# Making the first feed-forward layer's seven weight operands during attention, on ScalarE and GpSimd, instead of at the start of the feed-forward layer

## The chip, the cores and the metric

The kernel runs on one core of a Trainium2 chip. The metric is the device time of one execution in microseconds (us), lower is better. The core's engines work from queues of their own, each strictly in order: TensorE (PE, with its weight loads PEld), VectorE (DVE), ScalarE (ACT), GpSimd (POOL), and SyncE (SP), which here issues nearly all DMA transfers.

## The reference, cut to what matters

One transformer block on 2048 rows of width 512 in fp32: a modulated layer norm, an attention with 32 heads of 16 in four segments of 512 rows (softmax inside the segment plus a linear memory read from the earlier segments), and a feed-forward layer of width 1792.

```python
h = _layernorm(x, axis=-1) * (1 + ca) + sa
x = x + ga * _A_ref(h, A_wq, A_wk, A_wv, A_wo, A_beta)
h = _layernorm(x, axis=-1) * (1 + cb) + sb
x = x + gb * _B_ref(h, B_w1, B_b1, B_w2, B_b2)     # (relu(h @ w1 + b1) ** 2) @ w2 + b2
```

## The kernel before, in words

Precision: each fp32 operand of the large products is split into a rounded part "hi" (type fp32r) and the rest "lo" = value - hi, and a product is three matmuls: hi*hi, hi*lo, lo*hi. A split costs one copy (hi, on ACT) and one subtraction (lo, on DVE or POOL).

Stages. First W_q, W_k and W_v are loaded and split. Then 16 attention units u (four segments s times four groups of eight heads) are worked on: projections (`qk`, `vproj`), a first pass over the scores that finds row maxima (`a_quad`, whose maxima are read by the DVE line 854), a second pass with the exponentials (`b_quad`: ACT line 1035, causal zeroing on POOL line 1022, the product with V on PE line 1077), the linear memory (`mem`), and at the end of each unit a normalization (`norm`, DVE lines 1126 to 1129). The finished output of segments 0 to 2 goes to DRAM; that of segment 3 stays in the SBUF tile `X1L` (four blocks of 512 columns per partition). `X1L` is also where the raw W_q is loaded at the very start; between the two uses it holds nothing. Projecting the attention output (`wo_tile`, lines 1173 to 1208) and the second layer norm (`ln2`) follow, for segments 0 to 2 in between the units of the last segment.

The feed-forward layer runs over the four segments, and in each over seven pairs p of 128-wide blocks of the 1792 hidden columns. Its first product is done with Winograd's form of Strassen's scheme: seven block products instead of eight (`ffn1`, PE line 1470, twelve matmuls of 128x256 for each pair of block products), for which the 2x2 blocks A11, A12, A21, A22 of W1's pair are made into seven operands: A11, A12, A22 and the sums S1 = A21+A22, S2 = S1-A11, S3 = A11-A21, S4 = A12-S2. Each of the seven is split into hi and lo. The seven operands of a pair fill one slot of 1792 KB of the pool "w1", which has two slots. In segment 0 `load_w1` makes them: two loads of 256 KB (SP line 1382), four sums on POOL (line 1398), four copies on ACT (line 1405), four subtractions on DVE (line 1407), and a store of the finished slot to DRAM (`w1_dram`, SP line 1416). In segments 1 to 3 `fetch_w1` (line 1420) reads a finished slot back. W2's blocks are loaded, multiplied by the output gate on POOL (line 1429) and split (ACT line 1430, DVE line 1432) by `load_w2`, also in segment 0 only. The second product is `ffn2` (PE lines 1534 to 1536), whose input is squared and split on ACT and DVE (lines 1506 to 1518).

Order. The Python code makes a list of nodes (`op`, `act`, `dve`, `pe`, `sp`), each with an engine, the nodes that it follows and the buffers that it takes (`get`) and gives back (`put`). The table `ORDER` gives for each engine the sequence in which its nodes are issued, by node number. `Plan.run` only turns this into one emission order; semaphores between engines come from the tiles that the instructions share. `N_FFN` stands for the point where attention's tiles are freed and those of the feed-forward layer are laid over them.

Of the kernel before, what the change touches and what calls it, by code (L numbers as in the profile page):

```python
# [17 lines left out]
P = 128  # L18
# [39 lines left out]
8-16 3 17-33 86 94 34-35 88 36-39 96 111 40-43 105 123 44 117 45-76 171 77 161 172 162-163 173-174 164 175 165-167 176  # L58
168 177-178 328-329 214 330-331 215 333 216 749 217 334 231 335 754 336 239 219-220 252 221-222 487 266 488-489 273
260 490 197 492 198 236 245 493-494 199 242 200 495 202-203 257 248 204-205 357 263 613-615 278 285 276 616 281 371  # L60
288 618 293 619 269 620 378 365 432 621 386 297 383 301 298 764 435 299 304 362 308 368 311 320 316 374 392 516 759
521 558 321 389 437 444 322 561 403 440 768 324 769 447 770 395 771 524 530 452 773-774 537 775 527 776 684 411
456-458 533 545 413 405 460 551 642 687 419 467 463 877 937-938 475 647 939 470 940 656 650 421 427 479-481 429 563
942 542 943 570 944 573 945 578 801 548 802-804 566 653 806 554 807 663 671 808-809 659 582-584 586 483 818 593 819
589 820 677 601 821 1012 835 823 849 824 596 825-826 843 1072 668 1073-1074 880 846 1075 674 1362 605 883 689 1077 692
1078 680 1079 856 870 1080 606 867 696 607 699 840 708 704 1147 712 709-710 852 715 1207 970 1208 719 1209-1210 727
722 1212-1213 864 1214 1015 1215 861 978 873 991 609 731 1005 886 732-733 984 893 1018 896 889 999 735 901 1357 1352
981 1002 905-906 975 909 912 907 996 916 1367 987 919 1105 1113 928 924 1116 929 1008 1119 1150 1021 930 1153 1024
1028 932 1371-1372 1110 1031 1373 1036 1374 1126 1285 1040 1134 1044 1041-1042 1051 1059 1376 1122 1377 1047 1140 1378
1054 1379 1282 1240 1063 1288 1064-1065 1137 1421 1067 1156 1422 1159 1423-1424 1245 1131 1163 1426-1427 1171 1254  # L70
1428 1143 1429 1166 1404-1405 1248 1261 1406 1269 1407 1251 1175-1177 1179 1409 1272 1186 1410 1182 1411 1275 1257
1412 1438 1540-1541 1446 1189 1542-1543 1266 1480 1194 1545-1546 1452 1483 1547-1548 1278 1449 1198-1200 1291 1443
1675-1676 1202 1459 1677 1298 1678 1473 1301 1960 1955 1467 1680-1681 1464 1294 1682 1306 1455 1683 1470 1615 1573
1310-1311 1314 1810 1317 1811 1587 1812 1321 1813 1324 1312 1333 1476 1329 1815 1489 1816 1492 1817-1818 1581 1594
1334 1584 1970 1335 1578 1496 1486 1602 1499 1337 1504 1965 1508 1512 1618 1509 1750 1515 1510 1599 1519 1522 1621
1590 1605 1527 1608 1531 1708 1722 1753 1532 1624 1716 1631 1533 1756 1634 1974 1713 1627 1975 1611 1976 1729 1719
1977 1535 1639 1643-1644 1725 1647 1645 1743 1650 1979 1654 1980 1737 1981 1657 1885 1982 1740 1662 1666-1668 1759
1734 2003 1843 2004 1888 1766 2005 1746 2006 1851 1670 1769 2008-2009 1774 2010 1864 2011 1854 2132 1878 2133 1762
1857 2134-2135 1869 2079 2137 1778-1780 1848 1782 2138 1789 2139 1872 1860 2140 2037 2020-2023 1797 2051 1785
2025-2026 1875 1792 2027-2028 2045 1881 1801 2058 2072 1802-1803 2063 1894 2256 2048 1897 2257 1901 2258 2042 1904  # L80
2259 1805 1909 2261 2069 2262 2054 2263 2066 2182 2264 2203 1913-1915 1917 2187 2380 1924 2381 2193 1932 2382 1920
2383 1927 2190 2385 2075 2386 2161 2196 1936 2166 2082 2387-2388 2175 2085 1937-1938 2169 2089 2092 1891 2101 2097
1940 2105 2102-2103 2108 2112 2115 2172 2327 2120 2522 2124-2126 2178 2285 2299 2296 2128 2525 2532 2526-2528 2206
2209 2535 2213 2199 2536 2542 2537 2306 2293 2216 2538 2545 2290 2221 2311 2546 2552 2547-2548 2225-2227 2229 2320
2236 2555 2562 2556-2557 2232 2244 2239 2558 2565 2317 2302 2566 2602 2567-2568 2409 2417 2414 2248-2250 2330 2423
2337 2605-2606 2572 2333 2345 2314 2607-2608 2575 2340 2252 2323 2576 2612 2577-2578 2430 2420 2438 2349-2351 2444
2353 2356 2615 2582 2616-2618 2585 2360 2441 2363 2586 2368 2435 2426 2587 2643 2588 2622 2647 2372-2374 2454 2457
2461 2625-2627 2447 2464 2376 2469 2655 2592 2628 2473-2475 2477 2484 2480 2595-2596 2451 2487 2492 2597 2632 2598
2496-2498 2635 2651 2500 2636-2638 2662 2672 2692 2682 2665-2666 2685 2667 2686 2695-2697 2687 2668 2885 2688 2698
2882 2886 2883-2884 2675-2676 2888 2887 2905 2677-2678 2911 2906-2908 3046 2910 2909 3044-3045 3048 3050 3043 2928  # L90
# [3 lines left out]
3086 3022 3024 3087 3025 3153 3091-3092 3154 3090 3378 3155 3157 3089 3093 3156 3159 3094 3097-3098 3096 3370 3158  # L94
3095 3102 3177 3174 3176 3175 3105 3108 3179 3374 3099 3178 3180 3201 3196 3302 3301 3197 3195 3300 3305 3198-3199
3306 3200 3218 3217 3216 3304 3303 3312 3220 3318 3307 3310 3219 3314 3221-3222 3317 3238 3237 3239-3240 3308 3321
3241 3316 3319 3323 3320 3322 3327 3324 3243 3242 3259 3326 3260 3258 3330 3325 3261 3329 3263 3328 3331 3334 3262
3382 3338 3280 3282 3264 3335 3279 3281 3333 3332 3283 3336 3284 3339 3337 3342 3340 3344 3413 3410 3285 3346 3639
3341 3411-3412 3348 3343 3414-3415 3350 3345 3635 3354 3347 3416 3362 3432 3436 3433 3349 3431 3351 3434 3631 3355
3353 3435 3437 3352 3453 3452 3454 3457 3365 3627 3455 3359 3356 3560 3456 3458 3474 3558 3475 3473 3559 3562 3479  # L100
3476 3567 3563 3557 3569 3564 3497 3571 3477-3478 3561 3565 3494 3574 3496 3573 3576 3575 3495 3500 3577 3499 3580
3515 3520 3498 3578-3579 3582 3584 3581 3517 3516 3588 3585 3518 3583 3519 3587 3521 3536 3586 3590 3537 3591 3538
# [287 lines left out]
def block_kernel(ctx, tc, x, wq, wk, wv, wo, beta, w1, b1, w2, b2, c, wmod, out):  # L390
# [868 lines left out]
    def h2_ops(s, at):  # L1259
# [20 lines left out]
        for j, name in enumerate(BO):  # L1280
# [311 lines left out]
```

## Time and profile before

| | us |
|---|---|
| median of 3 runs | 802.03 (799.05, 802.03, 803.28) |
| the profiled execution's own time | 803.49 |
| its span, first to last instruction | 801.8 |
| PE busy in the span | 764.7 (95%) |
| DVE, ACT, POOL busy | 624.3 (78%), 445.9 (56%), 302.1 (38%) |
| mean granted TensorE clock | 0.989 |

The shares are means over the whole span. The parts of it that the following speaks of are, in us from the start of the span: the last of the projections' weights, then attention until about 450, segment 0 of the feed-forward layer from 450 to 550, segments 1 to 3 from 550 to 790, and the last output transfer until 802. A row of a table of stretches gives, for each engine, its busy time in that stretch and in brackets its instructions, then the granted clock, the mean busy share of the DMA engines and what they moved. A row of the waits reads "engine tile line <- what ended the wait: us in total, times, longest". A row of groups reads "line engine operation out<-in shape xcount | busy us, mean ns of one | idle time before". A row of one line gives minimum, median and maximum of the duration in ns and the first and last start.

### The profile page before, as it was taken

To read this page: it belongs to the slowest core of one execution; us is meant where nothing else is said; L and a number is where in the kernel's file an instruction comes from. 1 tells how busy PE (TensorE), PEld (TensorE's weight loads), DVE (VectorE), ACT (ScalarE), POOL (GpSimd) and SP (SyncE) were. 2 spreads that over 40 slices of the span, in tenths; PEclk is the share of its full clock that TensorE was granted. 3 is DMA by queue.
4 is the path that set the end of the run, shared out by engine and by line. 5 is a ranking of instruction groups with operands and counts; after the bars stand their busy time and mean duration, and the time that the engine had idled before them with its cause. 6 is when DMAs were issued, how large, how long until landed. Compare 5 with 4: busy or idle time off the path is not lost. (4 is left out here: it accounts for less than half of the span.)

```text
span 801.8 us, 18015 instructions
## 1 busy us (share of the span) xinstructions
PE 764.7 (95%) x6649; PEld 599.8 (75%) x6649; DVE 624.3 (78%) x1619; ACT 445.9 (56%) x1001; POOL 302.1 (38%) x372
## 2 busy tenths in 40 slices
PE   8999999999999999999999898899999999999993
PEld 8886667655877677775666576778998889889882
DVE  5488768788988787999898899999865875657351
ACT  2659767789869986868657545556212321221110
POOL 4735524657636774355132564564002020000000
PEclk9999999999999999999999999999999999999997
DMA  9563661323504333335531455677554463455504
GB/s 297 174 162 97 191 183 56 95 61 85 157 15 116 85 80 84 83 97 153 142 105 51 132 169 216 217 261 301 189 184 160 139 227 120 184 197 184 191 7 183
DMA packets 55345, 116.81 MB, mean 146 GB/s; under 512 B 8277, under 2 KB 25433, under 8 KB 51674
## 3 DMA queue, kind: packets, MB, share of 16 engines
q1 hardware_dynamic: 55106, 115.53, 45.4%
q8 instruction: 53, 0.87, 0.5%
q14 instruction: 34, 0.28, 0.1%
q10 hardware_dynamic: 152, 0.13, 0.1%
HBM read 68.45 MB, written 20.19 MB: 111 GB/s over the span
## 5 line engine op out<-in xcount | busy, mean ns | idle before, releaser
L854 DVE CUSTOM_DVE_ANT_0 ba<-ba,msk 128x384 f32<-128x384 f32 (+2 forms) x384 | 192.1, 532 | 26.5 <-PE ba L849 17.4
L1035 ACT ACTIVATE pt<-bpb 128x512 f32<-128x512 f32 x320 | 172.8, 610 | 27.6 <-PE bpb L1018 23.9
L1470 PEld LDWEIGHTS bh<-H2o,w 128*128 128x128 f32 x1176 | 155.9, 189 | 22.7 <-DVE w L1407 5.0
L1470 PE MATMUL bh<-H2o,w 128*128 128x256 f32 x1176 | 163.6, 283 | 7.6 <-DVE w L1407 3.2
L1022 POOL TENSOR_SCALAR_AFFINE_SELECT pt<-pt 128x512 f32<-128x512 f32 x128 | 81.4, 655 | 120.5 <-ACT pt L1035 78.3
L742 PE MATMUL bqk<-HT,WQK 64*128 64x512 f32 x720 | 103.3, 396 | 0.2
L1516 ACT CAST rr<-xx 128x512 fp32r<-128x512 f32 x56 | 34.5, 620 | 100.8 <-DVE xx L1506 65.3
L1077 PE MATMUL bpv<-pt,VT 128*32 128x512 f32 (+3 forms) x1024 | 82.1, 441 | 3.4 <-POOL pt L1022 3.0
L1018 PE MATMUL bpb<-ST 64*128 64x256 f32 (+2 forms) x512 | 80.3, 353 | 1.4 <-ACT phi L785 0.4
L849 PE MATMUL ba<-ST 63*128 63x256 f32 (+2 forms) x512 | 75.6, 346 | 1.4 <-ACT oraw L1101 0.7
L742 PEld LDWEIGHTS bqk<-HT,WQK 64*128 64x128 f32 x720 | 68.9, 185 | 9.2 <-DVE sg L778 0.6
L1018 PEld LDWEIGHTS bpb<-ST 64*128 64x128 f32 x512 | 51.2, 187 | 26.5 <-issue 5.9
L849 PEld LDWEIGHTS ba<-ST 63*128 63x128 f32 x512 | 49.6, 186 | 22.3 <-DVE mx L854 4.5
L1535 PE MATMUL bpf<-w,rr 128*128 128x512 f32 x160 | 63.0, 394 | 1.6 <-DVE w L1432 1.6
L1534 PE MATMUL bpf<-w,rr 128*128 128x512 f32 x160 | 63.5, 397 | 0.0
L1536 PE MATMUL bpf<-w,rr 128*128 128x512 f32 x160 | 62.8, 392 | 0.7 <-DVE rr L1518 0.7
L1077 PEld LDWEIGHTS bpv<-pt,VT 128*32 128x32 f32 x1024 | 27.3, 109 | 40.3 <-issue 28.9
L815 PE MATMUL bv<-WVO,HT 64*128 64x512 f32 x384 | 54.5, 397 | 0.4 <-ACT WVO L716 0.2
L854 DVE DVE_READ_ACCUMULATOR2_ANT mx<- 128x1 f32 x384 | 54.3, 141 | 0.0
L1518 DVE TENSOR_TENSOR rr<-xx,rr 128x512 fp32r<-128x512 f32 x56 | 42.8, 769 | 12.9 <-ACT rr L1516 12.7
L893 DVE TENSOR_REDUCE mx<-ac 128x4 f32<-128x1024 f32 x32 | 38.9, 1216 | 11.4 <-POOL ac L890 11.3
L1270 POOL TENSOR_TENSOR tt<-h2raw 128x512 f32<-128x512 f32 x8 | 11.9, 1492 | 93.9 <-ACT h2raw L1236 93.9
(175 smaller groups left out, 1439.7 us busy)
## 6 DMA issues: line engine op xcount, KB each, us to landing
w<-w1d SPq DMA_DIRECT2D x21, 1792.0 KB
ST<-sg SPq DMA_DIRECT2D x192, 128.0 KB
w1d<-w SPq DMA_DIRECT2D x7, 1792.0 KB
wr<-in_B_w SPq DMA_DIRECT2D x28, 256.0 KB
xt<-in_A_x SPq DMA_DIRECT2D x16, 256.0 KB
wm<-in_w_mod SPq DMA_DIRECT2D x16, 256.0 KB
xw<-in_A_x SPq DMA_DIRECT2D x16, 256.0 KB
o_dram<-on SPq DMA_DIRECT2D x12, 256.0 KB
```

The costliest lines, as they stand in the source:

```text
L742: nc.tensor.matmul(bank(banks[w]), W3(w, k, x, cols.start, cols.stop)[r], HT[r, y, k], start=turn == k == i == 0, stop=turn == 1 and k == ...
L815: nc.tensor.matmul(bank(banks[t]), HT[r, x, k, (t2 + t) * P:(t2 + t + 1) * P], WVO[r, k, y], start=turn == k == i == 0, stop=turn == 1 and ...
L849: nc.tensor.matmul(dst[:, c0:c0 + n], ST[b:b + 63, 0, sl, qt * P:(qt + 1) * P], ST[b:b + 63, 1, sl, :n], start=True, stop=True)
L854: nc.vector.tensor_tensor_reduce(i, i, msk[:, 512 - n:], scale=1.0, scalar=-3e38, op0=ALU.add, op1=ALU.max, accum_out=o)
L1018: nc.tensor.matmul(dst, ST[b:b + 64, 1, sl, kb * P:(kb + 1) * P], ST[b:b + 64, 0, sl, q0:512], start=True, stop=True)
L1022: nc.gpsimd.affine_select(out=ap, in_=ap, pattern=[[0, ap.shape[1]], [1, P]], compare_op=ALU.is_ge, fill=0.0, base=0, channel_multiplier=-1)
L1035: ns = [act(512, lambda j=j: nc.scalar.activation(buf("PPP"[n], pt)[:, i + j], bank(keys[j]), AF.Exp, scale=0.25), pr[slot] + 0.01 + 0.001 ...
L1077: nc.tensor.matmul(bank(o)[32 * hq:32 * hq + 32, q0:q0 + src.shape[1]], v[:, a:a + 32], src, start=start, stop=stop, tile_position=(0, 32 ...
L1470: nc.tensor.matmul(pb(i), A[:, x, kk], B[:, y, kk], start=kk == j == 0, stop=kk == 1 and j == 2)
L1534: nc.tensor.matmul(q, rh, wh, start=(i == 0), stop=False)
L1535: nc.tensor.matmul(q, rh, wl, start=False, stop=False)
L1536: nc.tensor.matmul(q, rl, wh, start=False, stop=(i == NF - 1))
```

## The change

`load_w1` is gone. `make_w1(p, ...)` is called for all seven pairs ahead of the attention's nodes, and its nodes are placed among those of attention by the new `ORDER`. It works in `X1L`: blocks 0 and 1 hold the pair's two raw loads, blocks 2 and 3 hold hi and lo of the operands being split. For each pair: two loads of 256 KB, four copies on ACT (three of 512 columns, one of 256), four subtractions on POOL (formerly DVE), four sums on POOL (of 256 columns, in place), and four stores to `w1_dram`, of two, one, two and two operands (512, 256, 512 and 512 KB). One raw buffer ("wx") and one output buffer ("wy") exist, so each split waits for the store of the one before, and each pair for the last split of the pair before. In segment 0, `fetch_w1(p, 0, ...)` now reads each slot back, as in the other segments. The normalization of the last segment, which writes `X1L`, waits for all stores. The order of the operands within a slot is changed (S3 ahead of S1). All five sequences in `ORDER` are new; only the node numbers at W1's place and the sequence differ, and no other work is added or taken out.

```diff
 ORDER = {
     "PE": """
...
-             "w1": 2, "w2": 5, "p1": 1, "u2": 2, "u3": 1, "tt": 3, "S": 1}
+             "w1": 2, "w2": 5, "p1": 1, "u2": 2, "u3": 1, "tt": 3, "wx": 1, "wy": 1}
...
+    AO = ("A11", "A12", "A22", "S3", "S1", "S2", "S4")
+    def make_w1(p, pr):
+        raw = [X1L[:, i].rearrange("p (k n) -> p k n", k=KD) for i in (0, 1)]
+        out_ = X1L[:, 2:4].rearrange("p a n -> p (a n)").bitcast(F32R)
+        wx = ("wx", p)
+        ld = [sp(lambda i=i: nc.sync.dma_start(raw[i], w1[:, (2 * p + i) * P:(2 * p + i + 1) * P].rearrange("(k p) n -> p k n", p=P)),
+                 pr, 1 << 18, after=[q for c in range(4) for q in WN[0, c]], get=[("wx", wx)]) for i in (0,)]
...
+        def split(i, a, b, src, deps, put):
...
+            h = act(n, lambda: nc.scalar.copy(flat(0), src), t, sbuf=True, after=deps, get=[("wy", wy)], put=put)
+            l = op("POOL", 1.24 if n == 512 else 0.72, lambda: nc.gpsimd.tensor_tensor(flat(1), src, flat(0).bitcast(F32), op=ALU.subtract), t + 0.07,
+                   after=[h], put=put)
+            W1D[p].append(sp(lambda: nc.sync.dma_start(w1_dram[p][:, :, a:b], view().bitcast(F32)), t + 0.18, n << 10, after=[h, l], put=[wy]))
...
+        def sum_(t, dst, x, y, f, deps):
+            return op("POOL", 0.72, lambda: nc.gpsimd.tensor_tensor(dst, x, y, op=f), pr + 0.07 * t, after=deps)
+        g1 = split(0, 0, 2, whole(0), [ld[0]], [wx])
+        g2 = split(1, 2, 3, blk(1, 1), [ld[1]], [wx])
+        n1 = sum_(12, blk(1, 1), blk(1, 0), blk(1, 1), ALU.add, g2)
+        n2 = sum_(13, blk(1, 0), blk(0, 0), blk(1, 0), ALU.subtract, [n1])
+        n3 = sum_(14, blk(0, 0), blk(1, 1), blk(0, 0), ALU.subtract, [n2, *g1])
+        n4 = sum_(15, blk(0, 1), blk(0, 1), blk(0, 0), ALU.subtract, [n3])
+        split(2, 3, 5, whole(1), [n2, n3], [wx])
+        split(3, 5, 7, whole(0), [n4], [wx])
...
-        ks = [op("DVE", 0.84, lambda j=j: norm(j), p_fin + 0.02 + 0.001 * j, after=[n, n_gate], put=[b[j]]) for j in (0, 1)]
+        ks = [op("DVE", 0.84, lambda j=j: norm(j), p_fin + 0.02 + 0.001 * j, after=[n, n_gate, *(W1L if last else [])], put=[b[j]]) for j in (0, 1)]
...
+    for p in range(NF // 2):
+        make_w1(p, 7.05 + 2.57 * p)
+    W1L = [n for p in W1D for n in W1D[p]]
...
-    def load_w1(p, t0):
...
-            sn[o] = op("POOL", 0.92, lambda o=o, x=x, y=y, f=f: nc.gpsimd.tensor_tensor(blk[o](), blk[x](), blk[y](), op=f), us(t0 - 6 + 0.7 * i),
...
-            l = op("DVE", n / 960 + 0.07, lambda a=a, b=b, src=src: nc.vector.tensor_tensor(
-                w1slot(p, 0)[:, 1, a:b], src(), w1slot(p, 0)[:, 0, a:b].bitcast(F32), op=ALU.subtract), us(t0 - 4.5 + i), after=[h], put=put)
...
-        n = sp(lambda: nc.sync.dma_start(w1slot(p, s).bitcast(F32), w1_dram[p]), us(t0 - 12), 7 << 18, after=[W1D[p]], get=[("w1", key)])
+        n = sp(lambda: nc.sync.dma_start(w1slot(p, s).bitcast(F32), w1_dram[p]), us(t0 - 12), 7 << 18, after=[N_FFN, *W1D[p]], get=[("w1", key)])
...
     for p in range(NP):
-        load_w1(p, STEP * p)
+        fetch_w1(p, 0, STEP * p)
         load_w2(p, STEP * p)
```

More of the change, by code (lines that the diff above doesn't have):

```diff
@@ L222 @@
+2307 2667 2533 2532 2527 2531 2530 2070 2525 2677 2328 2526 2524 2687 2528-2529 2534 2523 2727 2431 2697 2737 2452
+2707 2747 2555 2717 2576 2757 2827 2785 2832 2787 2846 2786 2797 2828 2836 2817 2807 2837 2845 2859 2841 2854 2850
+2855 2863 2908 2864 2868 2886 2872 2882 2873 2881 2877 3174-3180 3431-3437 3688-3689 3392 3690-3691 3138 3386 3692
+3389 3649 3693-3694 3132 3652 3903 3906 3135 3900 3643 3909 3646 3395 3129
 """,
@@ L710, in block_kernel, with whole, blk @@
     clear(2, PR0 + 1.3, [n_w])
+    AO = ("A11", "A12", "A22", "S3", "S1", "S2", "S4")
+    w1_dram = [dram.tile([P, 2, 7, 2, P], F32, name=f"w1d{p}") for p in range(NF // 2)]
+    W1D = {}
+    def make_w1(p, pr):
[4 more added lines that the diff above has]
+                 pr, 1 << 18, after=[q for c in range(4) for q in WN[0, c]], get=[("wx", wx)]) for i in (0,)]
+        ld.append(sp(lambda: nc.sync.dma_start(raw[1], w1[:, (2 * p + 1) * P:(2 * p + 2) * P].rearrange("(k p) n -> p k n", p=P)),
+                     pr + 0.01, 1 << 18, after=[q for c in range(4) for q in WN[0, c]], soft=ld))
+        W1D[p] = []
+        def split(i, a, b, src, deps, put):
+            n, wy, t = (b - a) * 256, ("wy", p, a), pr + 0.14 + 0.5 * i
+            view = lambda: out_[:, :2 * n].rearrange("p (h j k n) -> p h j k n", h=2, j=b - a, k=2)
+            flat = lambda q: out_[:, q * n:(q + 1) * n]
+            h = act(n, lambda: nc.scalar.copy(flat(0), src), t, sbuf=True, after=deps, get=[("wy", wy)], put=put)
+            l = op("POOL", 1.24 if n == 512 else 0.72, lambda: nc.gpsimd.tensor_tensor(flat(1), src, flat(0).bitcast(F32), op=ALU.subtract), t + 0.07,
+                   after=[h], put=put)
+            W1D[p].append(sp(lambda: nc.sync.dma_start(w1_dram[p][:, :, a:b], view().bitcast(F32)), t + 0.18, n << 10, after=[h, l], put=[wy]))
+            return [h, l]
+        def whole(i):
+            return X1L[:, i]
+        def blk(i, j):
+            return X1L[:, i, 256 * j:256 * j + 256]
+        def sum_(t, dst, x, y, f, deps):
[8 more added lines that the diff above has]
+        split(3, 5, 7, whole(0), [n4], [wx])
@@ L1354, in block_kernel @@
     STEP = 10.44
-    W1N, W2N, W1D = {}, {}, {}
+    W1N, W2N = {}, {}
     W2LATE = {3: 0, 5: 1}
-    w1_dram = [dram.tile([P, 2, 7, 2, P], F32, name=f"w1d{p}") for p in range(NP)]
     def wraw(k):
@@ L1376, in w2slot @@
         return TL[k]
-    def load_w1(p, t0):
-        key, ks, sk = ("w1", p, 0), [("wr1", p, i) for i in (0, 1)], ("S", p)
-        raw = [lambda i=i: wraw(ks[i]).rearrange("p (k n) -> p k n", k=KD) for i in (0, 1)]
-        ld = [sp(lambda i=i: nc.sync.dma_start(raw[i](), w1[:, (2 * p + i) * P:(2 * p + i + 1) * P].rearrange("(k p) n -> p k n", p=P)),
-                 us(t0 - 9 + i), 1 << 18, after=[N_FFN], get=[("wr", ks[i])]) for i in (0, 1)]
-        def S():
-            if sk not in TL:
-                TL[sk] = FF["sb"].tile([P, 4, 2, P], F32, name="S", tag="S0")
-            return TL[sk]
-        blk = {"A11": lambda: raw[0]()[:, 0:2], "A12": lambda: raw[0]()[:, 2:4], "A21": lambda: raw[1]()[:, 0:2], "A22": lambda: raw[1]()[:, 2:4],
-               "S1": lambda: S()[:, 0], "S2": lambda: S()[:, 1], "S3": lambda: S()[:, 2], "S4": lambda: S()[:, 3]}
-        f1, f2 = ks
-        prev = None
-        sn = {}
-        for i, (o, x, y, f, put) in enumerate((("S1", "A21", "A22", ALU.add, []), ("S2", "S1", "A11", ALU.subtract, []),
-                                               ("S3", "A11", "A21", ALU.subtract, []), ("S4", "A12", "S2", ALU.subtract, []))):
-            deps = [sn[q] for q in (x, y) if q in sn] + [ld[int(q[1]) - 1] for q in (x, y) if q[0] == "A"]
-            uses = sorted({ks[int(q[1]) - 1] for q in (x, y) if q[0] == "A"})
-            sn[o] = op("POOL", 0.92, lambda o=o, x=x, y=y, f=f: nc.gpsimd.tensor_tensor(blk[o](), blk[x](), blk[y](), op=f), us(t0 - 6 + 0.7 * i),
-                       after=deps, get=[("S", sk)] if i == 0 else (), put=uses)
-        ends = []
-        for i, (a, b, src, n, deps, put) in enumerate(((0, 2, lambda: raw[0]().rearrange("p (j k) n -> p j k n", j=2), 512, [ld[0]], [f1]),
-                                                 (2, 3, lambda: raw[1]()[:, None, 2:4], 256, [ld[1]], [f2]),
-                                                 (3, 5, lambda: S()[:, 0:2], 512, [sn["S1"], sn["S2"]], [sk]),
-                                                 (5, 7, lambda: S()[:, 2:4], 512, [sn["S3"], sn["S4"]], [sk]))):
-            h = act(n, lambda a=a, b=b, src=src: nc.scalar.copy(w1slot(p, 0)[:, 0, a:b], src()), us(t0 - 5 + i), sbuf=True, after=deps,
-                    get=() if i else [("w1", key)], put=put)
-            l = op("DVE", n / 960 + 0.07, lambda a=a, b=b, src=src: nc.vector.tensor_tensor(
-                w1slot(p, 0)[:, 1, a:b], src(), w1slot(p, 0)[:, 0, a:b].bitcast(F32), op=ALU.subtract), us(t0 - 4.5 + i), after=[h], put=put)
-            if i == 0:
-                first = h
-            else:
-                first.outs.append(h)
-                h.left += 1
-            ends.append([h, l])
-        W1N[p, 0] = {"A11": ends[0], "A12": ends[0], "A22": ends[1], "S1": ends[2], "S2": ends[2], "S3": ends[3], "S4": ends[3]}
-        W1D[p] = sp(lambda: nc.sync.dma_start(w1_dram[p], w1slot(p, 0).bitcast(F32)), us(t0 + 1), 7 << 18, after=[q for e_ in ends for q in e_], put=[key])
```

293 lines of the change are left out of this document (146 added, 147 removed), and 17 rows, old and new, of the table ORDER.

## The prediction

> **What bounds the kernel now.** I first cut the span into stages, since the shares of the page mix them. One row is one stretch: its length, then busy time of PE, PEld, DVE, ACT and POOL, granted clock, DMA share, GB/s.
>
> ```profile
> 46.00:375.00 329.00, 321.36 (x3668) 227.33 (x3668) 279.67 (x919) 265.23 (x635) 180.36 (x229) 0.99 0.38 102
> 375.00:450.00 75.00, 74.54 (x618) 49.56 (x614) 65.85 (x184) 49.11 (x106) 22.30 (x37) 1.00 0.38 107
> 450.00:470.00 20.00, 16.31 (x116) 12.54 (x109) 17.58 (x33) 9.55 (x19) 11.53 (x11) 1.00 0.48 130
> 470.00:550.00 80.00, 71.28 (x426) 59.39 (x425) 78.13 (x128) 45.91 (x89) 45.19 (x42) 1.00 0.66 239
> 550.00:790.00 240.00, 237.52 (x1482) 212.64 (x1480) 157.42 (x308) 53.37 (x105) 17.09 (x13) 1.00 0.45 163
> ```
>
> PE is the bound everywhere but in one place. In attention (46 to 450) it idles 7.64 + 0.46 us of 404; in segments 1 to 3 of the feed-forward layer 2.48 us of 240. In segment 0 (450 to 550) it idles 3.69 + 8.72 = 12.4 us of 100, and from 470 on DVE is busy 78.13 of 80 us: that stage is VectorE's. The waits of PE between 450 and 560 say on what:
>
> ```profile
> PE bh L1470 <- DVE w L1407: 3.2, 4, 1.8
> PE bwot L1200 <- DVE X1L L1135: 2.1, 1, 2.1
> PE bwop L1175 <- DVE oT L1208: 1.6, 1, 1.6
> PE bpf L1535 <- DVE w L1432: 1.6, 1, 1.6
> PE bpf L1536 <- DVE rr L1518: 1.2, 3, 0.5
> PE bh L1470 <- DVE xx L1489: 1.1, 2, 0.9
> PE bh L1470 <- DVE H2o L1286: 0.8, 2, 0.5
> PE bh L1470 <- DVE u L1493: 0.6, 1, 0.6
> ```
>
> All eight end on DVE. 3.2 us are W1's subtractions (L1407) themselves, 3.7 us (L1135, L1208) the hand-over from the last attention unit, and 5.3 us other results queued on the full DVE. The groups of 450 to 550 that the change takes out of this stage (L1407, L1405, L1398), and one that stays:
>
> ```profile
> L1407 DVE TENSOR_TENSOR w<-wr,w 128x256 fp32r<-128x256 f32 (+1 forms) x14 | 11.2, 806 | 0.5 <-ACT w L1405 0.5
> L1407 DVE TENSOR_TENSOR w<-S,w 128x512 fp32r<-128x512 f32 x14 | 10.1, 729 | 0.0
> L1405 ACT CAST w<-S 128x512 fp32r<-128x512 f32 x14 | 8.6, 620 | 5.7 <-POOL S L1398 5.7
> L1405 ACT CAST w<-wr 128x512 fp32r<-128x512 f32 (+1 forms) x14 | 7.0, 515 | 4.9 <-DMA wr<-in_B_w 4.8
> L1398 POOL TENSOR_TENSOR S<-wr 128x256 f32<-128x256 f32 x14 | 12.1, 869 | 11.4 <-DMA wr<-in_B_w 7.5 <-DVE h2raw L1238 2.2 <-DVE w L1407 1.6
> L1398 POOL TENSOR_TENSOR S<-wr,S 128x256 f32<-128x256 f32 x7 | 7.0, 1006 | 0.3
> L1398 POOL TENSOR_TENSOR S<-S,wr 128x256 f32<-128x256 f32 x7 | 7.0, 1005 | 2.8 <-DMA wr<-in_B_w 2.5
> L1518 DVE TENSOR_TENSOR rr<-xx,rr 128x512 fp32r<-128x512 f32 x12 | 12.2, 1013 | 0.6 <-ACT rr L1516 0.6
> ```
>
> **The gain in segment 0.** DVE loses 11.2 + 10.1 = 21.3 us, ACT 15.6, POOL 26.1. Of DVE's 95.7 us some 74 are left for 100, less still if the POOL sums slow the rest (L1518's mean is 1013 ns here; over the whole run its median is 685):
>
> ```profile
> L1518 DVE TENSOR_TENSOR rr<-xx,rr x56: 676/685/1787, 481.3 to 782.0; 128x512 fp32r<-128x512 f32 x56
> L778 DVE TENSOR_TENSOR sg<-bqk,sg x32: 679/691/693, 31.6 to 372.7; 128x512 fp32r<-128x512 f32 x32
> ```
>
> At 74%, DVE is about as loaded as in segments 1 to 3 (157.42 of 240, 66%), where PE idles 1%. So I take: the 3.2 us vanish; the 5.3 us shrink to 1.0 (1% of 80 us, rounded up for the W2 blocks still made here), gain 4.3; the 3.7 us of hand-over keep 3.0, since their chain (normalization, transposition, copy, subtraction) stays, and only lines waiting behind L1407 or slowed by L1398 get quicker, gain 0.7. Sum 8.2 us. Bounds: 3.2 if only the direct waits go, 12.4 if all idle time goes. What is late next there is PE itself.
>
> **W1 fetched in segment 0.** Seven stores of 1792 KB and fourteen loads leave the stage, seven fetches of 1792 KB come; less DMA than before in it.
>
> ```profile
> L1382 SPq DMA_DIRECT2D wr<-in_B_w x14: 368/379/459, 447.2 to 539.2; - x14
> L1470 PEld LDWEIGHTS bh<-H2o,w x1176: 186/188/193, 468.3 to 779.0; 128*128 128x128 f32 x196
> 756.00:762.00 6.00, 6.00 (x38) 5.29 (x37) 1.43 (x3) 1.62 (x3) 0.00 (x0) 1.00 0.87 323
> ```
>
> Around the last fetch 323 GB/s were moved, so 1.835 MB take 5.7 us. The first raw load could be issued at 447.2, as attention's tiles came free; a fetch from there lands by about 455, and the first weight load of L1470 is at 468.3. I cost the first fetch at nothing; if its slot lay over tiles freed 10 us later, it would cost about 2 us. The later five wait for a slot, as in segments 1 to 3, where PE's list names no DMA. Zero taken; ends zero and the second rival.
>
> **The price in attention.** The sequences show where the new nodes stand: counted against what ran beside them before, all 28 copies fall between 46 and 340 us, and the last POOL subtraction stands just ahead of the causal zeroing of 366.14. The rows for prices and cover (the two L1077 rows are PE's and PEld's waits of 46 to 375, L1022 the POOL group of that stretch):
>
> ```profile
> L611 POOL TENSOR_TENSOR HT<-lnf,HT x12: 1264/1279/1287, 70.8 to 285.6; 128x512 fp32r<-128x512 f32 x12
> L1398 POOL TENSOR_TENSOR S<-wr x14: 728/784/1181, 457.6 to 544.1; 128x256 f32<-128x256 f32 x14
> L1022 POOL TENSOR_SCALAR_AFFINE_SELECT pt<-pt 128x512 f32<-128x512 f32 x103 | 64.9, 649 | 74.6 <-ACT pt L1035 52.6 <-PE bqk L742 9.0 <-issue 5.9
> PE bpv L1077 <- POOL pt L1022: 2.7, 4, 1.2
> PEld bpv L1077 <- POOL pt L1022: 7.7, 16, 1.4
> 170.00:210.00 40.00, 38.92 (x504) 24.01 (x497) 35.91 (x119) 38.26 (x89) 25.02 (x36) 0.96 0.31 88
> 250.00:290.00 40.00, 39.35 (x490) 25.74 (x489) 32.48 (x106) 38.66 (x90) 29.22 (x39) 1.00 0.29 74
> ```
>
> - POOL: 21 subtractions of 512 columns at 1.279 us (L611, same shape), 7 of 256 and 28 sums at 0.784 (L1398's median): 26.9 + 5.5 + 22.0 = 54.3 us. POOL goes from 180.36 to 235 us of 329, 55% to 71%. Its queue is in order, and behind each new instruction stand zeroings of exponentials (L1022) that L1077 reads. The new work fills 54.3/329 = 16.5% of the time, so 103 zeroings lose on average half of 1.28 us in 16.5% of cases, 10.9 us in all; 20 of the 103 were waited for by PE or its weight loads before, so a fifth reaches PE: 2.1 us. Ends: zero (the sequence may put the new work into the 74.6 us in which POOL sat idle ahead of L1022) and all 10.9.
> - ACT: 21 copies at 0.62 us and 7 at about 0.4 (L1405: 515 mean over both sizes): 15.8 us, 265.23 to 281 of 329. Two stretches have no room: 3 copies (1.6 us) fall into 170 to 210, where ACT has 1.7 us left, and 4 (2.3 us) into 250 to 290, where it has 1.3. The overflow there is 1.0 us; I take 0.9, ends zero and the 3.9 us of all seven.
> - SP and DMA: 42 issues of 0.379 us are 16 us of a queue that carries the operand copies for the score products; each store waits for its subtraction, and all issues behind it wait too. The new traffic, 3.7 + 12.8 MB at 323 GB/s, is 51 us of wire in 329. PE's list of 46 to 375 names no DMA, so slack is there; I take 0.3, ends zero and 3.
> - The last segment's normalization waits for the last store. Its first start was 380.6; the last store follows 366.14 by 1.28 + 0.38 us of work and issue and 1.6 us of wire (512 KB at 323 GB/s), near 370. Ten us of cover: zero. Were that gone, DVE would stand with the maxima (L854) behind it, and PE after them.
>
> ```profile
> 366.14 2.94 POOL L1022 TENSOR_SCALAR_AFFINE_SELECT pt<-pt 128x512 f32<-128x512 f32 x3 [0.87 <-ACT pt L1035]
> L1129 DVE TENSOR_TENSOR X1L<-bfin,dn x8: 423/424/425, 380.6 to 456.4; 128x256 f32<-128x256 f32 x8
> L1128 DVE TENSOR_TENSOR dn<-dn,omg x32: 174/176/1269, 88.1 to 455.7; 128x16 f32<-128x16 f32 x32
> ```
>
> - POOL against DVE: L1518 (both inputs in SBUF, one shape) spreads from 676 to 1787 ns, L778 (one input in PSUM) stays within 679 to 693. In attention nearly all of DVE's time is on PSUM inputs; the exposed line is L1128, 176 ns at the median and 1269 at most. PE's list has no wait on its chain there, so: zero. The Trainium skill's page "SBUF — State Buffer", section "Who interferes with whom", speaks against the change here: a VectorE instruction with two SBUF inputs and a GpSimd instruction that reads SBUF exclude each other for a whole instruction. The two ranges above agree with it. By it some 24 of the L1128 would each meet a subtraction in 16.5% of cases and lose 0.64 us, an estimate of 2.5 us on DVE; if PE took all of that, the sum would come out at 799.6 and not 797.1.
> - The new sequences themselves: no row prices them. PE's switches between operand shapes are as many as before (174 against 175 by the two tables). Zero, and part of the range.
>
> Sum: -8.2 + 2.1 + 0.9 + 0.3 = -4.9 us. The profiled execution took 803.49, 1.5 above the median; against it the change gives 798.6, against the median of 802.03 it gives **797.1**. Half a per cent, about what a measurement here can tell from no change, is 4.0 us: faster means below 798.0, slower above 806.0.
>
> **The rivals.**
> - *All of the idle time goes and attention hides everything* (near 791): 12.4 less 1 to 2. For it: POOL's 74.6 idle us ahead of the zeroings, and DVE's relief. Against it: the hand-over chain and the full ACT stretches.
> - *The gain turns into a wait for fetched slots* (802 to 803). A slot is free only after its pair's seven products, and then takes 5.7 us, with 512 KB of W2 loads (1.6 us) sharing the wire. If each of the five later fetches comes 1.0 us late, 5 us are lost and nothing is left of the 4.9; at 1.2 us it is 803. Against it: in segments 1 to 3 the same slots do, though without W2's loads.
> - *POOL sets attention's pace* (slower, near 807). The queue is in order and VectorE, ACT and PE are all over 80% busy beside it. If every one of the 56 new instructions held PE up by 0.22 us, 12.3 us would be lost in place of 3.3, less 8.2: 806. It decides above that; at 0.15 us each there is no change. For it: from 170 to 210 and from 250 to 290 POOL is already at 63% and 73%. Against it: only 2.7 us of PE's waits name POOL now.
> - *No gain for want of cause*: if PE's idle time came from its own sequence and not from DVE, moving DVE's work would do nothing. All eight rows name DVE, so this has no chance of its own.
>
> **How the numbers follow.** Forecast (793 to 799.5) 0.44, all idle time goes 0.18, fetch or another wait takes the gain 0.20, POOL paces 0.18. Four fifths of the forecast's share and all of the first rival lie below 798.0: 0.53. The second rival, the rest of the forecast and a fifth of the last give 0.33 for no change, and 0.14 is left for slower. The range 789.5 to 805 leaves out the best of the first rival and most of the last.
>
> **What would show it.** From 450 to 550 in the new profile: no L1407 and L1398 groups, DVE near 70 us, L1518's mean near 750 ns, PE's idle time 4 to 5 us, of which 2 to 3 at L1135 and L1208. From 46 to 375: POOL near 235 us, ACT 281, PE's idle time 10 to 11 instead of 7.6, waits on L1022 up by 2. The forecast is wrong if PE's list names a DMA of w before L1470, if attention's idle time rises above 13, or if segment 0 still idles over 8.

## The result, and the profile after

The changed kernel takes 792.17 us (median of 4, 791.11 to 792.94) against 801.93 for the kernel before beside it: ratio 0.9882, 95% interval 0.9852 to 0.9913, 9.8 us faster. Forecast were 4.9 us less, 797.1. The sign and the range held, but twice the forecast was gained, and the time lies below the 793 to 799.5 of the forecast itself. That it stayed inside the range at all is in part luck: errors of opposite sign were in the sum. The profiled execution took 792.94, its span is 790.9.

The stages of the changed kernel (columns as in the prediction):

```profile
46.00:375.00 329.00, 316.81 (x3556) 229.87 (x3552) 270.35 (x891) 266.50 (x643) 220.44 (x275) 0.98 0.51 150
375.00:450.00 75.00, 74.03 (x650) 48.70 (x650) 69.03 (x193) 51.96 (x111) 29.46 (x41) 0.98 0.37 111
450.00:470.00 20.00, 18.45 (x164) 12.74 (x156) 15.51 (x35) 12.40 (x26) 6.80 (x8) 1.00 0.73 218
470.00:550.00 80.00, 78.62 (x504) 70.57 (x504) 67.85 (x125) 41.79 (x82) 32.62 (x25) 1.00 0.61 226
550.00:790.00 240.00, 231.72 (x1434) 206.94 (x1433) 152.08 (x295) 46.53 (x93) 12.18 (x8) 0.99 0.46 164
```

Between 450 and 550 PE now idles 1.55 + 1.38 = 2.9 us instead of 12.4. But from 46 to 375 it idles 12.2 us instead of 7.6, and the DMA share there is 0.51 instead of 0.38. Stretches at fixed times hide that the work inside them has moved, so the two kernels are better compared at events: the last product with V (the end of attention), the last matmul, the end of the span. From the timelines of PE, before and after (start, length, line):

```profile
449.11 2.36 PE L1077 MATMUL bpv<-pt,VT 128*32 128x512 f32 x32
...
788.68 0.39 PE L1536 MATMUL bpf<-w,rr 128*128 128x512 f32 x1
```

```profile
457.77 2.36 PE L1120 MATMUL bpv<-pt,VT 128*32 128x512 f32 x32
...
781.49 0.39 PE L1539 MATMUL bpf<-w,rr 128*128 128x512 f32 x1
```

| | before | after | difference |
|---|---|---|---|
| start to the end of attention | 451.5 | 460.1 | +8.7 |
| from there to the last matmul (the feed-forward layer) | 337.6 | 321.8 | -15.9 |
| from there to the end of the span (last stores) | 12.7 | 9.0 | -3.7 |
| span | 801.8 | 790.9 | -10.9 |

So attention lost far more than the 3.3 us that I had put down, the feed-forward layer gained twice the 8.2, and 3.7 us came from a place that I had not looked at. The waits of PE after, from 440 to 550:

```profile
PE bwot L1243 <- DVE X1L L1178: 1.3, 1, 1.3
PE bwop L1218 <- DVE oT L1251: 0.7, 2, 0.5
PE blnq L599 <- DVE xh L595: 0.6, 1, 0.6
PE bh L1473 <- DVE H2o L1328: 0.2, 1, 0.2
```

Of the eight rows of before the hand-over (2.0 of 3.7 us) and 0.2 us on H2o are left; no row names a DMA, so the fetches are in time. The heaviest of PE's waits from 0 to 375, where before no row named a DMA after 46:

```profile
PE bfin L1155 <- ACT oraw L1144: 2.2, 2, 1.4
...
PE ba L892 <- DMA ST<-sg: 1.7, 1, 1.7
PE bmod L558 <- DMA wm<-in_w_mod: 1.4, 1, 1.4
PE bat L957 <- DVE mx L897: 1.1, 3, 0.8
PE bpv L1120 <- POOL pt L1065: 1.1, 3, 0.5
```

PE now waits for the operand copies of the score products (ST<-sg) and for W_mod's loads; for POOL's zeroings it waits less than before (1.1 us instead of 2.7).

### The profile page after: what moved, and what is told of

It is laid out like the page before. It is cut to its first block, busy times and chain, and to the rows that moved or that the text cites. A ratio compares the mean times of both kernels' runs of the same rounds, so it can differ in the third digit from the quotient of the medians.

```text
span 790.9 us, 18000 instructions
## 1 busy us (share of the span) xinstructions
PE 762.8 (96%) x6649; PEld 607.2 (77%) x6649; DVE 603.3 (76%) x1591; ACT 441.7 (56%) x1001; POOL 327.9 (41%) x400
## 5 line engine op out<-in xcount | busy, mean ns | idle before, releaser
L897 DVE CUSTOM_DVE_ANT_0 ba<-ba,msk 128x512 f32<-128x512 f32 (+2 forms) x384 | 192.2, 531 | 35.9 <-PE ba L892 29.5
L1473 PE MATMUL bh<-H2o,w 128*128 128x256 f32 x1176 | 159.6, 282 | 0.3 <-DVE H2o L1328 0.2
L1120 PE MATMUL bpv<-pt,VT 128*32 128x512 f32 (+3 forms) x1024 | 84.0, 450 | 1.5 <-POOL pt L1065 1.1
L892 PE MATMUL ba<-ST 63*128 63x256 f32 (+2 forms) x512 | 79.1, 351 | 3.6 <-DMA ST<-sg 1.7
L785 PEld LDWEIGHTS bqk<-HT,WQK 64*128 64x128 f32 x720 | 74.0, 186 | 7.4 <-DVE tm L1037 0.5
L892 PEld LDWEIGHTS ba<-ST 63*128 63x128 f32 x512 | 51.3, 188 | 30.9 <-ACT pt L1078 7.2
L858 PE MATMUL bv<-WVO,HT 64*128 64x512 f32 x384 | 54.3, 397 | 0.2 <-ACT WVO L759 0.2
L1521 DVE TENSOR_TENSOR rr<-xx,rr 128x512 fp32r<-128x512 f32 x56 | 42.4, 762 | 12.3 <-ACT rr L1519 12.0
L830 POOL TENSOR_SCALAR e<-e 128x512 f32<-128x512 f32 x24 | 35.7, 1488 | 21.6 <-ACT e L826 13.9
```

Of the source, the lines that this page charges most:

```text
L785: nc.tensor.matmul(bank(banks[w]), W3(w, k, x, cols.start, cols.stop)[r], HT[r, y, k], start=turn == k == i == 0, stop=turn == 1 and k == ...
L858: nc.tensor.matmul(bank(banks[t]), HT[r, x, k, (t2 + t) * P:(t2 + t + 1) * P], WVO[r, k, y], start=turn == k == i == 0, stop=turn == 1 and ...
L892: nc.tensor.matmul(dst[:, c0:c0 + n], ST[b:b + 63, 0, sl, qt * P:(qt + 1) * P], ST[b:b + 63, 1, sl, :n], start=True, stop=True)
L897: nc.vector.tensor_tensor_reduce(i, i, msk[:, 512 - n:], scale=1.0, scalar=-3e38, op0=ALU.add, op1=ALU.max, accum_out=o)
L1120: nc.tensor.matmul(bank(o)[32 * hq:32 * hq + 32, q0:q0 + src.shape[1]], v[:, a:a + 32], src, start=start, stop=stop, tile_position=(0, 32 ...
L1473: nc.tensor.matmul(pb(i), A[:, x, kk], B[:, y, kk], start=kk == j == 0, stop=kk == 1 and j == 2)
```

## The experiments

Every ratio below is against the kernel before, run on the same chip in the same set; the absolute times of different sets differ by a few us and are not compared. The time at which the last product with V starts is from one profiled execution of each.

**Run 1: does the work in attention cost it, or the new sequences?** The nodes stay in their places, but emit nothing for six of the seven pairs.

```diff
-            h = act(n, lambda: nc.scalar.copy(flat(0), src), ...
+            h = act(n, lambda: p == 0 and nc.scalar.copy(flat(0), src), ...      # likewise l, sums, loads, stores
-        n = sp(lambda: nc.sync.dma_start(w1slot(p, s).bitcast(F32), w1_dram[p]), ...
+        n = sp(lambda: nc.sync.dma_start(w1slot(p, s).bitcast(F32), w1_dram[0]), ...
```

> The changed kernel with its own sequences, but W1's operands are made for the first pair only; the loads, copies, subtractions, sums and stores of the other six pairs are left out and all pairs fetch the first one's store. Question: do the new instructions make attention longer (it ends 8.7 us later than before, at the last product with V), or do the new sequences? Theory (the work costs it): most of it goes, attention ends 6 to 9 us earlier than in the changed kernel and the time falls to 783 to 787. Rival (the sequences cost it): attention ends within 2 us of the changed kernel's, time 790 to 793.

Measured: ratio 0.9772 (0.9729 to 0.9814).

```profile
448.31 2.36 PE L1120 MATMUL bpv<-pt,VT 128*32 128x512 f32 x32
```

Attention ends 9.5 us earlier than in the changed kernel, a little more than the theory's 6 to 9, and 0.8 us earlier than before; the time is 784.5 us, as the theory has it. The new sequences cost attention nothing; W1's work there costs all of it.

**Run 2: VectorE's work put back.** Two more subtractions behind each of W2's fourteen, into a scratch tile.

```diff
+                for m in (D, D if i else D // 2):
+                    nc.vector.tensor_tensor(FF["scr"][:, :m], wraw(k)[:, :m], w2slot(p)[:, i, 0, :m].bitcast(F32), op=ALU.subtract)
```

> The changed kernel with 28 further subtractions of the former line 1407's sizes put back on VectorE in segment 0 of the feed-forward layer (two behind each of W2's fourteen, results unused; about 17 us of VectorE). Theory (relief of VectorE is what made segment 0 quicker): VectorE is over 95% busy from 470 to 550 again, PE idles 6 to 12 us there instead of 2.9, and the time rises by 5 to 11 us, to 797 to 803. Rival (the new sequences or the fetches did it): within 2 us of 792.

Measured: 1.0039 (1.0021 to 1.0057), some 13 us above the changed kernel's 0.987 to 0.988, more than the theory's upper end. Its stretch, and the heaviest of PE's waits from 440 to 560:

```profile
470.00:550.00 80.00, 68.89 (x423) 58.80 (x422) 72.88 (x131) 33.86 (x68) 31.78 (x24) 1.00 0.56 203
```

```profile
PE bh L1479 <- DVE xx L1498: 3.6, 4, 2.2
PE bh L1479 <- DVE u L1502: 3.5, 3, 1.9
PE bh L1479 <- DVE u L1498: 1.7, 2, 1.5
PE bpf L1545 <- DVE rr L1527: 1.5, 2, 0.9
```

PE idles 11.1 of 80 us, and from the end of attention to the last matmul the profile has 336.5 us, against 321.8 in the changed kernel and 337.6 before. The theory's direction holds, its picture of it does not: DVE is at 91%, not over 95%. The added instructions need not fill the engine; standing in the queue ahead of sums that PE waits for is enough.

**Run 3: the stores at the end.** In the sequences, output stores of early segments had been left to the end of SyncE's queue: after the last matmul it still issued 14 stores before, and 9 in the changed kernel (the eleven of the expectation are counted in the sequence, behind the last fetch; two of them got out earlier).

```diff
-  ... stores of segments 0 to 3 behind the last fetch of segment 3
+  ... the four stores of segment s (s = 0, 1, 2) behind the fifth fetch of segment s + 1; segment 3's at the end
```

> The changed kernel with only SyncE's sequence altered: the output stores of segments 0 to 2 each stand behind the fifth fetch of the following segment, instead of eleven stores behind the last fetch of all. Theory (the end after the last matmul is the time of the stores that pile up: 14 before, 11 after): the time from the last matmul to the end falls from 9.0 to 3 to 5 us and the kernel gains 4 to 6 us, 786 to 788. Rival (the end is set by the last tile's own store): no change, 791 to 793. Risk: a store that waits ahead of a fetch makes PE wait, then slower.

Measured: 0.9800 (0.9765 to 0.9834), about 6 us below the changed kernel's ratio. The end after the last matmul is 5.6 us in its profile instead of 9.0, a little over the theory's 3 to 5.

**Run 4: VectorE relieved without the change.** In the kernel before, line 1407 is left out for pairs 2 to 6.

```diff
+ ...      # w1slot: in segment 0 the tile of a slot is made once and kept
-            l = op("DVE", n / 960 + 0.07, lambda a=a, b=b, src=src: nc.vector.tensor_tensor(
+            l = op("DVE", n / 960 + 0.07, lambda a=a, b=b, src=src: p < 2 and nc.vector.tensor_tensor(
```

> The kernel before, with line 1407's subtractions left out for pairs 2 to 6 (20 of 28, about 15 us of VectorE; the slot keeps the low part of an earlier pair); sequences and all else as before. Theory (VectorE bounds segment 0): PE's idle time from 450 to 550 falls from 12.4 us to 5 to 8, time 794 to 798. Rival (the sequence itself spaces PE's work there, or POOL's sums and the loads do): at most 2 us, 800 to 802.

Measured: 0.9885 (0.9866 to 0.9905), 9 us, with POOL's sums, ACT's copies and the old sequences in place. All of it is in the feed-forward layer: 328.2 us from the end of attention to the last matmul, 9.4 less than before. That is 9.4 of the 15.9 us that the change gained there, for 20 of the 28 subtractions.

```profile
450.00:470.00 20.00, 16.31 (x118) 12.31 (x111) 18.05 (x33) 9.10 (x19) 11.41 (x12) 1.00 0.48 125
470.00:550.00 80.00, 77.52 (x491) 68.39 (x490) 68.72 (x121) 50.90 (x99) 51.38 (x47) 1.00 0.75 271
```

PE's idle time in the segment is 6.2 us, 6.2 less than before. With run 2, which takes back 14.8 of the 15.9 us, this shows that DVE's subtractions were what held segment 0. Whether taking POOL's sums and ACT's copies out gained something of its own wasn't separated.

**Runs 5 to 8: which part of W1's work costs attention?** The changed kernel itself, then without ACT's and POOL's instructions, without loads and stores (pairs 1 to 6), and without POOL's alone; each by the same kind of edit as run 1.

> The changed kernel itself, for comparison with the next three on one chip. Both theories: 0.985 to 0.991 of the kernel before.

> The changed kernel with W1's ACT copies and POOL subtractions and sums left out in attention; its 14 loads and 28 stores stay (they carry raw data). Without six of the seven pairs' work of every kind attention ended 9.4 us earlier than in the changed kernel. Theory A (the queues of ACT and POOL cost it): attention ends 6 to 9 us earlier than in the changed kernel, ratio to the kernel before 0.976 to 0.980. Theory B (transfers cost it: 16.5 MB on the wire and stores that hold SyncE's queue up): attention ends within 3 us of the changed kernel's, 0.985 to 0.990.

> The changed kernel with the copies, subtractions and sums of all pairs, but the loads and stores of pairs 1 to 6 left out; all pairs fetch pair 0's store. Theory A: attention ends within 3 us of the changed kernel's, ratio 0.985 to 0.990. Theory B: 6 to 9 us earlier, 0.976 to 0.980.

> The changed kernel without W1's 56 POOL instructions; copies on ACT, loads and stores stay. Theory POOL (its queue in order is what delays attention, two thirds of my predicted price): attention ends 4 to 8 us earlier than in the changed kernel, ratio 0.978 to 0.984. Theory ACT or transfers: within 3 us, 0.985 to 0.990.

| run | in attention | ratio (95%) | last product with V starts | PE idle | PE busy | windows |
|---|---|---|---|---|---|---|
| the kernel before | none | 1 | 449.11 | 8.1 | 397.4 | 2 |
| the changed kernel, first profile | all | 0.9882 (0.9852 to 0.9913) | 457.77 | 13.2 | 401.0 | 4 |
| 5, the changed kernel | all | 0.9870 (0.9833 to 0.9907) | 459.64 | 14.7 | 401.3 | 4 |
| 6 | transfers only | 0.9830 (0.9794 to 0.9865) | 458.03 | 14.5 | 399.9 | 5 |
| 7 | ACT and POOL only | 0.9786 (0.9750 to 0.9821) | 450.14 | 8.5 | 398.0 | 2 |
| 8 | transfers and ACT | 0.9826 (0.9792 to 0.9860) | 453.00 | 12.9 | 396.5 | 2 |
| 1 | nearly nothing | 0.9772 (0.9729 to 0.9814) | 448.31 | 8.1 | 396.6 | 2 |

PE's idle and busy time are from 46 us to the end of attention; the last column counts the windows of half TensorE clock in attention, of which the last section speaks.

Theory A, that the compute queues alone cost it, falls: with all of ACT's and POOL's work and no transfers, attention ends 9.5 us earlier than with both. By the ratios, at 803 us: nothing to compute alone 1.1 us, nothing to transfers alone 4.7, to both 7.9; taking the transfers out of the changed kernel gains 6.7, taking POOL's instructions out 3.5. The intervals are 6 us wide, so the shares are not exact. That transfers are the larger part is shown by run 7's time and by PE's idle time: 8.1 and 8.5 us without them, 12.9 to 14.7 with them, whether POOL or ACT work beside them or not.

Run 6 gained 3.2 us by its ratio, between the two theories' figures; its profiled execution was the slowest of its four (793.1, median 790.2). Run 8 met the theory of POOL in both figures, 0.9826 and 6.6 us earlier than run 5. But its profiled execution was the fastest of its four, and only 1.8 of the 6.6 us are idle time of PE; the other 4.8 are busy time, 3.4 of them two windows of half clock fewer. So beside the transfers POOL's instructions cost something, 3.5 us by the ratio; how much of it is theirs, and how much the clock's, stays open. PE's waits from 30 to 450 in run 7 begin with POOL and DVE and name no DMA:

```profile
PE bpv L1120 <- POOL pt L1065: 1.5, 5, 0.5
PE bat L957 <- DVE mx L897: 1.2, 3, 0.8
PE blnq L599 <- DVE xt L595: 0.9, 1, 0.9
PE bmr L985 <- DVE mx L897: 0.9, 1, 0.9
```

In run 6 two DMA stand first and fourth among them:

```profile
PE bmod L558 <- DMA wm<-in_w_mod: 2.1, 1, 2.1
...
PE ba L892 <- DMA ST<-sg: 1.5, 1, 1.5
```

**Run 9: the wire or the queue?** The same transfers at the same places, an eighth of the rows each.

```diff
+    m_ = lambda p: P if p == 0 else P // 8
-            ... nc.sync.dma_start(w1_dram[p][:, :, a:b], view().bitcast(F32)) ...
+            ... nc.sync.dma_start(w1_dram[p][:m_(p), :, a:b], view().bitcast(F32)[:m_(p)]) ...      # likewise the loads
```

> The changed kernel with the same 14 loads and 28 stores, at the same places of SyncE's queue and with the same waits, but for pairs 1 to 6 each moves only an eighth of its rows (all pairs fetch pair 0's store). Without the transfers attention ended 8 to 9 us earlier; this tells the wire from the queue. Theory wire (16.5 MB delay the operand copies and W_mod's loads): attention ends 5 to 9 us earlier than in the changed kernel, ratio 0.978 to 0.982. Theory queue (issue times and stores that wait for POOL hold back what stands behind them on SyncE): within 3 us, 0.985 to 0.989.

Measured: 0.9823 (0.9802 to 0.9844), the last product with V starts at 453.21, 4.6 to 6.4 us earlier than in the changed kernel's two profiles. That is between the two: by the ratios the bytes cost some 4 us, and some 3 remain over runs 1 and 7 for the 42 issues and their waits, a difference no larger than the intervals. PE's idle time to the end of attention is 9.8 us here, 1.7 over run 1, against 5.1 and 6.6 over it in the changed kernel's two profiles, so most of the idle time goes with the bytes. SyncE still waits for POOL's subtraction about as long as in the changed kernel, where the row has 18.9 us (its waits from 46 to 375; the line is the store's):

```profile
SPq L738 <- POOL X1L L736: 18.0, 8, 6.1
```

**Run 10: the stores moved to GpSimd's queue,** where nothing has to wait for the subtraction.

```diff
-            W1D[p].append(sp(lambda: nc.sync.dma_start(w1_dram[p][:, :, a:b], view().bitcast(F32)), ...
+            W1D[p].append(sp(lambda: nc.gpsimd.dma_start(w1_dram[p][:, :, a:b], view().bitcast(F32)), ...
```

> The changed kernel with the 28 stores issued from GpSimd's queue, behind the subtraction that they need, instead of SyncE's; same bytes. Theory queue: SyncE is 16 us of issues and 25 us of waits freer, attention ends 4 to 7 us earlier, ratio 0.979 to 0.983. Theory wire: no gain, 0.985 to 0.990; slower if issuing a store holds GpSimd up by more than a microsecond each.

Measured: 0.9946 (0.9915 to 0.9976), slower than the changed kernel by 6 us; attention's last product starts at 463.50. The theory of the queue fails as a remedy:

```profile
L736 POOL DMA_DIRECT2D w1d<-X1L x28: 652/706/845, 54.7 to 386.9; - x28
```

Each issue holds GpSimd 0.7 us, 20 us in all. Whether this alone makes the loss wasn't separated.

**Runs 11 and 12: the stores early, again, and in the kernel before.** The edit of run 3 in both kernels.

> The changed kernel with the output stores of segments 0 to 2 early in SyncE's sequence, as in the third run, timed again with more rounds beside the next kernel. Theory (piled-up stores make the end; first run: 5.6 us from the last matmul to the end instead of 9.0): ratio to the kernel before 0.978 to 0.984, against 0.987 and 0.988 for the changed kernel. Rival (it was chance): 0.986 to 0.990.

> The kernel before with the same edit alone: output stores of segments 0 to 2 behind the fifth fetch of the following segment. Theory: the end after the last matmul falls from 12.7 us to 5 to 6, and nothing else moves: 6 to 8 us faster, ratio 0.990 to 0.993. So 3.6 us of the change's gain came from where its new sequence happened to put these stores. Rival: no more than 2 us, 0.997 to 1.0.

Measured: run 11 0.9808 (0.9772 to 0.9844), 787.1 us; run 12 0.9922 (0.9898 to 0.9947), 796.1 us. The store lines before, after, and in run 11 (first and last start at the end):

```profile
L1547 SPq DMA_DIRECT2D out<-X x12: 426/640/799, 714.1 to 797.2; - x12
```

```profile
L1550 SPq DMA_DIRECT2D out<-X x12: 422/431/637, 695.5 to 787.0; - x12
```

```profile
L1552 SPq DMA_DIRECT2D out<-X x12: 337/430/823, 574.3 to 728.8; - x12
L1552 SPq DMA_DIRECT2D out<-X1L x4: 338/438/453, 782.6 to 783.9; - x4
```

Of SyncE's stores only the four of X1L, segment 3's, are left behind the last matmul. Taken from the last matmul to the last instruction, run 11's end is 5.6 us and run 12's 5.9, against 9.0 and 12.7. The edit is worth 6.3 us to the kernel before (the theory's 6 to 8), and with 14, 9 and 4 stores left the end is 12.7, 9.0 and 5.6 to 5.9 us. So the 3.7 us by which the change shortened the end go with the five stores that its new sequence let out earlier. Run 11 is the fastest version: its interval lies wholly below that of the changed kernel's first timing, though it meets that of run 5.

## Why the prediction was right or wrong, point by point

- *VectorE bounds segment 0, PE is late next:* right. Runs 2 and 4 show it from both sides.
- *The gain there, 8.2 us with 12.4 as the upper bound:* mis-sized; 15.9 were measured. The step that failed is the bound. I took PE's recorded idle time for all that VectorE could cost. Idle time in the two stretches fell by 9.5, and from 550 to the last matmul by 1.4 (239.07 - 237.52 before, 231.88 - 231.72 after). But stalls also sat inside the matmuls counted as busy. The group's row over the whole run, before and after:

```profile
L1470 PE MATMUL bh<-H2o,w 128*128 128x256 f32 x1176 | 163.6, 283 | 7.6 <-DVE w L1407 3.2 <-DVE xx L1489 1.1 <-DVE H2o L1286 0.8
```

```profile
L1473 PE MATMUL bh<-H2o,w 128*128 128x256 f32 x1176 | 159.6, 282 | 0.3 <-DVE H2o L1328 0.2 <-DVE xx L1492 0.2
```

  The same 1176 matmuls are busy 4.0 us less, and all of it is in segment 0: its 294 matmuls of this line are busy 44.0 us before (mean 288 ns) and 39.6 after (282). 9.5 + 1.4 + 4.0 are 14.9 of the 15.9. Taken over the whole feed-forward layer, from the end of attention to the last matmul, PE idles 14.0 us before and 3.1 after, and is busy for 323.6 and 318.7.
- *DVE near 70 us from 450 to 550, L1518's mean near 750 ns:* DVE came to 83.4, since the stretch now holds more of the layer's work (668 matmuls of PE in its two rows instead of 542), and L1518's successor L1521 to 770 ns:

```profile
L1521 DVE TENSOR_TENSOR rr<-xx,rr 128x512 fp32r<-128x512 f32 x13 | 10.0, 770 | 0.0
```

  PE hardly idles all the same. With run 2, where DVE at 91% held PE up, this speaks for what stands ahead of PE's operands in the queue, and against the share, as what counts.
- *The hand-over keeps 3.0:* 2.0 were left.
- *Fetches at nothing:* right; the second rival's wait, a DMA ahead of the first product, did not come.
- *POOL 2.1 us and ACT 0.9 in attention:* the size was about right (1.1 us alone in run 7, 3.5 on top of the transfers in run 8), the place was not: waits on the zeroings went down from 2.7 to 1.1 us instead of up by 2. Up to the end of attention POOL worked 49.6 us more and ACT 10.3, where 54.3 and 15.8 were reckoned.
- *Transfers 0.3 us:* the term that was worst. By the ratios they cost 4.7 us alone, and 6.7 on top of the rest. The step "PE's list of 46 to 375 names no DMA, so slack is there" failed: a list without such waits shows that the slack was enough for the load of then (DMA share 0.38), not how much is left for 16.5 MB more (0.51). I had the wire at 51 us of 329 in the text and drew nothing from it. The prediction's own sign, attention's idle time above 13 us, came, if barely: 13.2.
- *The granted clock:* no term of the sum. PE is busy 3.6 us longer to the end of attention with the same products (397.4 and 401.0), which is about what two more windows at half clock take (3.4).
- *The new sequences at nothing:* right for attention (448.31 against 449.11 in run 1), wrong for the end of the kernel, where they moved five stores and 3.7 us. I had not looked at SyncE's last entries, though the table was in the change.
- *The rivals:* the time met the first one (near 791), not its reason: attention hid little. POOL as the pacer, 12.3 us lost to it, has no support: alone with ACT it cost 1.1 us.
- *VectorE and GpSimd excluding each other in attention (the Trainium skill, "SBUF — State Buffer", "Who interferes with whom"), priced at zero:* not tested by itself; run 7, with all of POOL's work, leaves 1.1 us for this and all other costs of the compute. DVE's busy time to the end of attention is 346.1 us there and 344.4 in run 1, 1.7 us more, where the prediction's estimate was 2.5.

## What to carry to other kernels

Work moved out of a stage bound by one engine can gain more than the idle time of the stage's other engine shows, because stalls can also hide in time counted as busy (44.0 us against 39.6 for the same 294 matmuls); an ablation of the bounding engine's work (run 4) sizes it directly. Price transfers put beside a tuned stage by the bytes and the queue they share with short, urgent transfers: no wait in the profile before means only that slack was not used up. Look at the last entries of the transfer queue whenever sequences change: here the end was 12.7, 9.0 and 5.6 us with 14, 9 and 4 stores left to it.

## What the runs showed of the hardware that was not expected

The granted TensorE clock drops to half for short times in the middle of attention. Before, in one execution (stretch, PE busy, ..., clock):

```profile
100.00:110.00 10.00, 9.74 (x115) 7.03 (x116) 7.28 (x32) 7.76 (x16) 4.24 (x5) 0.83 0.58 189
103.00:105.00 2.00, 2.00 (x14) 0.76 (x8) 1.45 (x7) 1.14 (x3) 1.33 (x2) 0.50 0.00 0
```

The changed kernel:

```profile
100.00:110.00 10.00, 10.00 (x122) 6.88 (x115) 6.63 (x25) 8.61 (x21) 9.29 (x10) 0.83 0.62 200
170.00:180.00 10.00, 8.37 (x64) 3.75 (x64) 7.46 (x26) 7.06 (x16) 6.32 (x7) 0.66 0.19 58
370.00:380.00 10.00, 8.50 (x116) 4.42 (x108) 9.37 (x19) 8.88 (x19) 5.29 (x5) 0.83 0.31 107
```

A mean of 0.83 over 10 us is about 3.4 us at half clock, 0.66 twice that. The Trainium skill, "TensorE: Matmul & The Clock Gate", Part 1, gives windows of 3413 ns and half clock after an idle one; the length agrees. The 3.4 us just ahead of the drops hold no wholly idle window, but some with long gaps. First the second drop of the kernel before, then the three places of the changed kernel:

```profile
166.56:169.98 3.42, 1.94 (x32) 1.21 (x30) 2.99 (x13) 2.23 (x6) 2.67 (x4) 1.00 0.26 71
```

```profile
101.42:104.83 3.41, 3.41 (x52) 2.79 (x55) 3.34 (x12) 3.18 (x10) 3.25 (x5) 1.00 0.72 221
169.69:173.10 3.41, 1.66 (x22) 1.17 (x22) 2.14 (x8) 2.62 (x8) 2.73 (x4) 1.00 0.27 91
371.07:374.48 3.41, 2.29 (x30) 1.34 (x30) 2.85 (x6) 3.28 (x7) 0.63 (x1) 1.00 0.45 160
```

PE was busy for 1.94, 1.66 and 2.29 us of 3.4 ahead of the drops near 170, 173 and 374, but all the time ahead of the one at 104.8, so what sets them off stays open. The kernel before had two such windows in attention, in each of three profiles with its sequences (this one, runs 4 and 12); the changed kernel had four in this profile and in run 5, and six and five in runs 3 and 11; runs 1, 7 and 8 had two. Two more take at most 3.4 us. Of the 8.7 us that attention lost 5.1 are idle time of PE (13.2 instead of 8.1), and the other 3.6, longer busy time, are about what these two windows explain. Whether the changed kernel's longer waits bring the further windows was not tested. Where they fall differed between executions of the changed kernel, which makes single profiles of attention's end uncertain by a few us.
